# Where the second batch's filter sums run, how its second transform stage is fed, and in which steps both stand

## The chip, the cores and the metric

The kernel runs on one core of a Trainium2 chip. The metric is device time in microseconds for one execution of the whole program; the chip holds only this work. The five engines of the core are TensorE (PE, with weight loads shown as PEld), VectorE (DVE), ScalarE (ACT), GpSimd (POOL) and SyncE (SP, which here only issues DMAs).

## The reference

Two operations follow each other. The first mixes along the sequence with a filter in the frequency domain, the second is a feed-forward block with hard-swish. All is float32.

```python
# x: (8, 3008, 256); filt_r, filt_i: (1505, 256)
X = np.fft.rfft(x, axis=1)
Y = X * (filt_r + 1j * filt_i)[None, :, :]
y = np.fft.irfft(Y, n=3008, axis=1).reshape(8 * 3008, 256)
# w_in: (256, 2048), w_out: (2048, 256)
h = y @ w_in
g = h * np.clip(h + 3.0, 0.0, 6.0) / 6.0
out = g @ w_out
```

## The kernel before

**The transform** is a two-factor one, 3008 = 47 x 64. For each of the 8 batches, five kinds of unit are run:

- `a_unit(b, c)`, eight per batch: the first stage. Input pieces (47 rows in each half of the partitions) are multiplied by the table `wa`. It takes two PSUM banks. ScalarE copies the result; `z_store` writes it to the DRAM tensor `z_d`.
- `t2_load(b, c)`, six per batch: SP loads a tile of four frequency groups back from `z_d`, 512 KB.
- `b_unit(b, i)`: the second stage, with a table as the stationary operand. It fills one PSUM bank for each i, 12 in a batch.
- `f_unit(b, i)` multiplies a bank by the filter (loaded by `table_load` into `ft`), giving `s1` and `s2`. `y_unit(b, i)` adds and subtracts these into `y`.
- `bi_unit(b, i)`, for two i at a time: the first inverse stage, into two banks; ScalarE copies them to the single `t3` buffer and `g_store` writes them to `g_d` from GpSimd's queue. Later `t4_load` reads `g_d`, and `n_unit(i, dh)` does the last inverse stage and writes tokens into the ring `xn`.

All of `a_unit`, `b_unit`, `bi_unit` and `n_unit` take their banks from the one pool `psF`, which has two, under the one tag `f`; they are taken in turn.

**The feed-forward block** runs over 47 blocks of 512 tokens, each in eight steps `p` over 256 of the 2048 hidden columns. It uses a seven-product scheme in place of eight products, with sums before and after. A step is a round of the last loop of the kernel: number i = 8 x block + p. In step i TensorE runs the seven up products of step i (line 575, through `product`) and the fourteen down matmuls of step i - 1 (line 651), interleaved by hand. VectorE's queue in a step is: `hswish(k, p, 1)` of the step before (line 625), the three sums of `g_sums` (632, 633, 635), the sums `up_2b` (601) and `up_3` (606), `hswish(k, p, 0)` (625), and then what the plan has put at this step's end. At the first and last step of a block five output sums come on top. Block 0 is done by plain products (`plain_up`, `plain_down`).

**The order** is written out by hand. `at(step, fn, ...)` puts a unit into the plan of a step. Units in `EARLY` (a, b, bi and n) stand after the first three up products of the step; everything else stands at the end of the step. Within one of these lists the order is that of the calls to `at`. `places(n)` gives the steps of batch n: `a_at`, `f_at`, `y_at` and `bi_at`. From the third batch on these are offsets to the batch's first block; for the second batch (n = 1) they are a list of their own, because its transform has to run in the steps 2 to 31, while block 0 to block 3 are worked on. Batch 0 is transformed before the loop starts.

**What is special in batch 1 before.** The first stage makes two half sums (h = 0, 1). From batch 2 on `a_sums` adds and subtracts them on VectorE ahead of the store. In batch 1 the halves are stored as they are, and `t2_sums` adds and subtracts them after the load, at the steps `sums_at`, two VectorE instructions for each of six tiles. The filter products of batch 1 are placed so that both operands of the `y` sums lie on the same partitions (`near(b)`): four products of 64 x 512, and the two sums run on GpSimd (lines 461 and 462). In the later batches there are three products (446 to 448) and the two sums run on VectorE (464 and 465).

Of the kernel before, what the change touches and what calls it, by code (L numbers as in the profile page):

```python
# [12 lines left out]
AXT = mybir.ActivationFunctionType  # L13
ALU = mybir.AluOpType
PSUM = bass.MemoryType.PSUM

# [12 lines left out]
P = 128  # L31
# [27 lines left out]
def _make_tables():  # L59
    a = np.arange(NA)  # L60
    c = np.arange(NC)
    wa = np.zeros((P, HC * 2 * KH + 16))
    wai = np.zeros((P, HC, TOK))
    start = np.zeros((P, 2 * P))
    for h in range(2):
        for k in range(KH):
            th = 2 * np.pi * ((a * k) % NA) / NA

            at = k // 4 * 4 + (0, 2, 1, 3)[k % 4]
            for j in range(HC):  # L70
                tw = 2 * np.pi * (((a * NC + h * HC + j) * k) % N) / N
                wa[h * 64:h * 64 + NA, j * 2 * KH + at] = np.cos(tw)
                wa[h * 64:h * 64 + NA, j * 2 * KH + KH + at] = -np.sin(tw)
            start[h * 64:h * 64 + NA, P + 4 * k + h] = np.cos(th)
            start[h * 64:h * 64 + NA, P + 4 * k + 2 + h] = -np.sin(th)
    wb = np.zeros((P, KH, P))
    wi = np.zeros((P, 4, NC))
    wf = np.zeros((P, 2, 64))
    re, im = slice(0, NC), slice(NC, P)
    for k in range(KH):  # L80
        for q in range(64):
            f, sign = (k + NA * q, 1.0) if q < 32 else (NA * (q - 31) - k, -1.0)
            th = 2 * np.pi * ((c * f) % N) / N
            cs, sn = np.cos(th), np.sin(th)
            if f in (0, NF - 1):
                sn = np.zeros(NC)
            wb[re, k, q], wb[im, k, q] = cs, sign * sn
            wb[re, k, HALF + q], wb[im, k, HALF + q] = -sn, sign * cs

    for q in range(64):  # L90
        g, sign = (q, 1.0) if q < 32 else (31 - q, -1.0)
        co, si = (f([2 * np.pi * ((j * g) % NC) / NC for j in range(HC + 1)]) for f in (np.cos, np.sin))
        ab = np.concatenate([co, np.zeros(HC - 1) if q == 63 else si[1:HC]])
        wi[q, 3], wi[HALF + q, 3] = ab, sign * ab

        at = g % 2 * 32 + (q // 2 if q < 32 else 16 + (q - 32) // 2)
        wi[at, 0], wi[HALF + at, 0] = ab, sign * ab
        cs, sn = (np.array([f(2 * np.pi * ((j * g) % NC) / NC) for j in range(HC)]) for f in (np.cos, np.sin))
        if g % 32 == 0:
            sn = np.zeros(HC)  # L100
        for r in range(0, P, HALF):
            wf[r:r + 32, g % 2, at % 32], wf[r + 32:r + 64, g % 2, at % 32] = cs, sn
            wf[r:r + 32, g % 2, 32 + at % 32], wf[r + 32:r + 64, g % 2, 32 + at % 32] = -sign * sn, sign * cs
        wi[q, 1], wi[HALF + q, 1] = ab, -ab
        wi[q, 2], wi[HALF + q, 2] = sign * ab, sign * ab
    start[:, :P] = np.eye(P)
    for j in range(HC):
        for h in range(2):
            to = slice(h * NA, (h + 1) * NA)
            for k in range(KH):  # L110
                m = 2.0 if k else 1.0
                th = 2 * np.pi * ((a * k * NC + outer(j, h) * k) % N) / N
                cs, sn = m * np.cos(th), m * np.sin(th)
                s = -1.0 if h else 1.0
                if j:
                    wai[k, j, to], wai[32 + k, j, to] = cs, -sn
                    wai[64 + k, j, to], wai[96 + k, j, to] = -s * sn, -s * cs
                else:
                    wai[h * 64 + k, j, to], wai[h * 64 + 32 + k, j, to] = cs, -sn
    direct = np.zeros((P, TC, ND))  # L120
    n = np.array([i * NC + outer(j, h) for j in range(NJ + 1) for h in range(2) for i in range(NA)])
    for k in range(KH - TC, KH):
        for q in range(64):
            th = 2 * np.pi * (((k + NA * q if q < 32 else NA * (q - 31) - k) * n) % N) / N
            direct[q, k - KH + TC], direct[HALF + q, k - KH + TC] = 2 / N * np.cos(th), -2 / N * np.sin(th)
    f = np.float32
    return wa.astype(f), (wai / N).astype(f), wb.astype(f), wi.astype(f), wf.astype(f), start.astype(f), direct.astype(f)
# [3 lines left out]
def kernel(  # L131
# [42 lines left out]
    psO = pool("psO", 1, space=PSUM)  # L174

    wa = const.tile([P, HC * 2 * KH + 16], FP32, name="wa")
    wf = const.tile([P, 2, 64], FP32, name="wf")
    wai = const.tile([P, HC, TOK], FP32, name="wai")
    wi = const.tile([P, 4, NC], FP32, name="wi")
    xs = const.tile([P, 3, XC, D], FP32, name="xs")  # L180
# [207 lines left out]
        nc.vector.tensor_tensor(out=t[:, :, 1, :], in0=t[:, :, 0, :], in1=ps, op=ALU.subtract)  # L388
        nc.vector.tensor_tensor(out=t[:, :, 0, :], in0=t[:, :, 0, :], in1=ps, op=ALU.add)  # L389

    def t2_sums(b, c):
        t = st["t2", b, c]
        u = st["t2", b, c] = t1p.tile([P, XC // 2, 2, D], FP32, name="t1")
        nc.vector.tensor_tensor(out=u[:, :, 0, :], in0=t[:, :, 0, :], in1=t[:, :, 1, :], op=ALU.add)
        nc.vector.tensor_tensor(out=u[:, :, 1, :], in0=t[:, :, 0, :], in1=t[:, :, 1, :], op=ALU.subtract)

    def z_store(b, c, q=nc.gpsimd):
        t = st.pop(("t1", b, c))[0]
        for g in range(2):
# [3 lines left out]
                            t[p0:p0 + KH, :, :, :].rearrange("p j s d -> p (j s d)"))  # L403


    def t2_load(b, c):
        t = t2p.tile([P, TC, D], FP32, name="t2").rearrange("p (v s) d -> p v s d", v=2)
        nc.sync.dma_start(t.rearrange("p v s d -> p v (s d)"),
                          z_d[b, ts(c, TC)].rearrange("(v k) r c s d -> (k r c) v (s d)", k=2))
        st["t2", b, c] = t  # L410
# [2 lines left out]

    def b_unit(b, i):
        c, r = divmod(2 * i, TC)
        if b:
            t = st.pop(("t2", b, c))
            ps = [bank(b) for k in range(2)]
            for s_ in range(2):
# [6 lines left out]
            return  # L426
        ps = bank(b).rearrange("p (u d) -> p u d", u=2)
        for u in range(2):
            nc.tensor.matmul(ps[:, u, :], st["wb", b, c][:, r + u, :],  # L429
                             st["t2", b, c][:, r + u, :], start=True, stop=True)  # L430
        st["ps", b, i] = ps

    def f_unit(b, i):
# [5 lines left out]
        s1, s2 = (pool_.tile([P, 512], FP32, name=n).rearrange("p (u d) -> p u d", u=2) for n in (n1, n2))  # L439

        re, im = slice(0, HALF), slice(HALF, P)
        if near(b):
            for s, part, to, x_ in (s1, re, re, re), (s1, re, im, im), (s2, im, re, im), (s2, im, im, re):
                nc.vector.tensor_tensor(out=s[to], in0=ps[x_], in1=f[part], op=ALU.mult)  # L444
        else:
            nc.vector.tensor_tensor(out=s1, in0=ps, in1=f, op=ALU.mult)
            nc.vector.tensor_tensor(out=s2[re], in0=ps[re], in1=f[im], op=ALU.mult)
            nc.vector.tensor_tensor(out=s2[im], in0=ps[im], in1=f[re], op=ALU.mult)
        st["y", b, i] = s1, s2


    def near(b):
        return b == 1

    def y_unit(b, i):
        s1, s2 = st["y", b, i]
        y = yp.tile([P, 2, D], FP32, name="y") if b else rp.tile([P, 512], FP32, name="r", tag="r").rearrange(
            "p (u d) -> p u d", u=2)
        re, im = slice(0, HALF), slice(HALF, P)
        if near(b):  # L460
            nc.gpsimd.tensor_tensor(out=y[re], in0=s1[re], in1=s2[re], op=ALU.subtract)
            nc.gpsimd.tensor_tensor(out=y[im], in0=s1[im], in1=s2[im], op=ALU.add)
        else:
            nc.vector.tensor_tensor(out=y[re], in0=s1[re], in1=s1[im], op=ALU.subtract)
            nc.vector.tensor_tensor(out=y[im], in0=s2[re], in1=s2[im], op=ALU.add)
        st["y", b, i] = y


# [272 lines left out]
    with tc.manual_schedule():  # L741
# [116 lines left out]
                kinds[first[n] - 7 + d] = kind  # L858

        N_AT = {"a": ((2, 4), (2, 4), (6, 6)), "A": ((4, 5), (1, 1), (4, 5)), "B": ((2, 3), (1, 1), (2, 3))}  # L860
        N_FIRST = {0: ((3, 4),), 1: ((), (2, 2), (3, 3)), 2: ((2, 2),), 3: ((1, 1),)}
        in_block = {}
        for i in range(2, len(chunks)):
            in_block.setdefault(token(i)[0] // BLK, []).append(i)
# [18 lines left out]

        def places(n):
            if n == 1:
                f_at = [12, 13, 14, 15, 19, 20, 21, 22, 26, 27, 28, 29]
                return list(range(2, NB + 2)), f_at, [f + 1 for f in f_at], [16, 17, 23, 24, 30, 31]
            k = first[n] * NP
            a_at = [k - 7 * NP + i for i in (1, 3, 5, 7, 9, 11, 13, 15)]
            f_at, y_at, bi_at = ([k - (5 - 2 * r) * NP + i for r in range(2) for i in p]  # L890
                                 for p in ((2, 3, 6, 7, 12, 13), (4, 5, 10, 11, 14, 15), (8, 14, 16)))
            return a_at, f_at, y_at, bi_at

        sums_at = [11, 11, 17, 18, 25, 25]
        prev = None
        for n in range(1, B):
            a_at, f_at, y_at, bi_at = places(n)
# [7 lines left out]
                elif n > 1:  # L905
                    at(max(prev[c + NB - 3], s - 6), x_load, n, c)
            for c in range(NT):
                s = (sums_at[c - TB] if n == 1 else f_at[2 * (c - TB)]) + 1 if c >= TB else a_at[-1] + 1
                at(s, t2_load, n, c)
                if n == 1:  # L910
                    at(sums_at[c], t2_sums, n, c)
                s = f_at[2 * (c - FB) + 1] + 1 if c >= FB else a_at[-1 if n > 1 else 3] + 1
                at(s, table_load, n, c)
            for i in range(NU):
                if i % 2 == 0:
                    at(f_at[i], b_unit, n, i)
                    at(bi_at[i // 2], bi_unit, n, i)
                    at(bi_at[i // 2], g_store, n, i)
                at(f_at[i], f_unit, n, i)
                at(y_at[i], y_unit, n, i)  # L920
            prev = a_at


# [97 lines left out]
```

## Time and profile before

| | before |
|---|---|
| median of 7 runs | 2721.74 us (2718.7 to 2722.64) |
| time of the profiled execution | 2721.74 us |
| its span, first to last instruction | 2720.0 us, clock 0.998 |
| PE busy | 2682.2 us (99%) |
| DVE busy | 2033.5 us (75%) |
| ACT busy | 1305.7 us (48%) |
| POOL busy | 407.4 us (15%) |
| DMA | 185.83 MB, mean 68 GB/s |

The span leaves 1.74 us of the profiled execution's time outside the first and last instruction. PE's busy share says only that a matmul was in flight; whether TensorE ran at its rate is seen from the length of a step. Idle time of the other engines costs nothing unless TensorE then waits for them.

### The profile page before, as it was taken

The numbers are of one execution on the slowest core, as the hardware profiler recorded it, in microseconds if no ns is written. First come the engines' busy times: TensorE is split into PE (matmuls) and PEld (weight loads), VectorE is DVE, ScalarE is ACT, GpSimd is POOL, SyncE is SP. The second block draws the span as 40 slices with busy tenths as digits, with TensorE's granted clock in tenths as the row PEclk, the third lists the DMA queues.
The fourth block names the chain that finished last, engine by engine and source line by source line (L and its number), as shares of the span: only waits on it lengthen the run. The fifth ranks groups of instructions, "written<-read, shape, count | busy, mean of one in ns | idle before, by whom it ended". The sixth has DMA issues, their size and how long they took to land.

```text
span 2720.0 us, 49001 instructions
## 1 busy us (share of the span) xinstructions
PE 2682.2 (99%) x18894; PEld 2358.7 (87%) x18894; DVE 2033.5 (75%) x3503; ACT 1305.7 (48%) x2614; POOL 407.4 (15%) x622
## 2 busy tenths in 40 slices
PE   8899999999999999999999999999999999999998
PEld 6577788988888888988889888988888988899997
DVE  7968767787777876778767787678776778766665
ACT  3344454445544454444454445445444454445443
POOL 2432311101211011110111001211012110000000
PEclk9999999999999999999999999999999999999999
DMA  8742223211232113321133212331123321110000
GB/s 232 205 113 53 58 78 86 75 42 48 79 87 73 43 49 87 87 74 36 48 88 95 68 35 51 96 89 58 36 52 98 89 65 28 43 30 17 19 9 16
DMA packets 105062, 185.83 MB, mean 68 GB/s; under 512 B 23609, under 2 KB 63225, under 8 KB 104513
## 3 DMA queue, kind: packets, MB, share of 16 engines
q1 hardware_dynamic: 87071, 137.99, 18.3%
q0 software_dynamic: 17152, 44.22, 6.2%
q8 instruction: 150, 2.46, 0.4%
q14 instruction: 83, 0.68, 0.1%
q10 hardware_dynamic: 606, 0.49, 0.1%
HBM read 110.67 MB, written 71.93 MB: 67 GB/s over the span
## 4 chain that ended last, share of the span: by engine, by line
PE 92%; DVE 5%; DMA 1%; issue 0%; ACT 0%; SPq 0%; POOL 0%; DVEq 0%; POOLq 0%
PE po L651 42%; PE al L575 23%; PE be L575 17%; PE psn L529 4%; PE psf L476 2%; PE psf L379 2%; PE psf L422 1%; DVE g L625 1%; DVE s L444 1%; PE po L346 1%; DVE g L632 0%; PE po L429 0%; DMA out_dram<-o 0%; DVE y L271 0%; DVE y L282 0%
## 5 line engine op out<-in xcount | busy, mean ns | idle before, releaser
L651 PEld LDWEIGHTS po<-w_all,g 128*128 128x128 f32 x10304 | 1362.3, 191 | 160.9 <-issue 41.7
L651 PE MATMUL po<-w_all,g 128*128 128x128 f32 x10304 | 1406.2, 276 | 4.6 <-DVE g L625 4.5
L620 ACT ACTIVATE r<-h,half_c 128x512 f32<-128x512 f32 x736 | 531.0, 722 | 348.8 <-DVE h L601 336.7
L625 DVE SCALAR_TENSOR_TENSOR g<-r,h 128x512 f32<-128x512 f32 x736 | 513.5, 698 | 212.2 <-ACT r L620 197.5
L575 PE MATMUL al<-xt,w_all 128*128 128x256 f32 x2208 | 660.7, 381 | 4.9 <-DVE h L606 4.3
L575 PE MATMUL be<-xn,w_all 128*128 128x256 f32 x1472 | 437.8, 379 | 0.0
L601 DVE TENSOR_TENSOR h<-be,s 128x512 f32<-128x512 f32 x368 | 254.2, 691 | 225.5 <-PE be L575 213.2
L575 PEld LDWEIGHTS al<-xt,w_all 128*128 128x128 f32 x2208 | 335.2, 192 | 7.4 <-DVE h L606 5.6
L575 PEld LDWEIGHTS be<-xn,w_all 128*128 128x128 f32 x1472 | 279.7, 190 | 37.9
L615 ACT ACTIVATE h<-al 128x256 f32<-128x256 f32 x368 | 141.0, 383 | 336.6 <-PE al L575 336.6
L606 DVE TENSOR_TENSOR h<-al,s 128x256 f32<-128x256 f32 x368 | 156.1, 424 | 160.9 <-PE al L575 159.7
L633 DVE TENSOR_TENSOR g<-g 128x512 f32<-128x512 f32 x368 | 255.0, 693 | 12.6
L596 ACT ACTIVATE s<-al 128x256 f32<-128x256 f32 x368 | 141.2, 384 | 206.2 <-PE al L575 204.2
L587 ACT ACTIVATE s<-be 128x256 f32<-128x256 f32 x368 | 141.1, 383 | 176.6 <-PE be L575 176.6
L575 PE MATMUL al<-xn,w_all 128*128 128x256 f32 x736 | 219.9, 381 | 0.5 <-ACT h L615 0.5
L575 PE MATMUL be<-xt,w_all 128*128 128x256 f32 x736 | 218.9, 379 | 0.0
L635 DVE TENSOR_TENSOR g<-g 128x256 f32<-128x256 f32 x368 | 169.7, 461 | 12.5
L586 ACT ACTIVATE s<-al 128x256 f32<-128x256 f32 x368 | 141.1, 383 | 71.4 <-PE al L575 71.3
L632 DVE TENSOR_TENSOR g<-g 128x256 f32<-128x256 f32 x368 | 164.3, 446 | 12.6
L402 POOL DMA_DIRECT2D z_tmp<-t x192 | 95.2, 503 | 452.2 <-DVE t L389 441.9
L575 PEld LDWEIGHTS be<-xt,w_all 128*128 128x128 f32 x736 | 139.8, 190 | 18.9
L496 POOL DMA_DIRECT2D g_tmp<-t x84 | 52.5, 630 | 645.0 <-ACT t L479 645.0
(142 smaller groups left out, 1852.4 us busy)
## 6 DMA issues: line engine op xcount, KB each, us to landing
g_tmp<-t POOLq DMA_DIRECT2D x96, 256.0 KB, 3.7
t<-g_tmp SPq DMA_DIRECT2D x188, 120.0 KB
t<-z_tmp SPq DMA_DIRECT2D x42, 512.0 KB
z_tmp<-t POOLq DMA_DIRECT2D x192, 96.0 KB, 4.0
out_dram<-o SPq DMA_DIRECT2D x321, 47.0 KB
xs<-in_x_dram SPq DMA_DIRECT2D x112, 128.0 KB
ft<-in_filt_r_dram SPq DMA_DIRECT2D x168, 64.0 KB
ft<-in_filt_i_dram SPq DMA_DIRECT2D x168, 64.0 KB
```

The source lines that it names most:

```text
L575: nc.tensor.matmul(ps, w_in[p][:, w, :], x, start=start, stop=stop, skip_group_check=True)
L586: nc.scalar.activation(out=s[:, 0, :], in_=al, func=AXT.Copy)
L587: nc.scalar.activation(out=s5, in_=be[:, 1, :], func=AXT.Copy)
L596: nc.scalar.activation(out=s[:, 1, :], in_=al, func=AXT.Copy)
L601: nc.vector.tensor_tensor(out=st["h"][0].rearrange("p (a n) -> p a n", a=2), in0=be, in1=s, op=ALU.add)
L606: nc.vector.tensor_tensor(out=st["h"][1][:, 256:512], in0=al, in1=s5, op=ALU.add)
L620: nc.scalar.activation(out=r, in_=st["h"][i], func=AXT.Relu, bias=half_c, scale=1.0 / 6.0)
L625: nc.vector.scalar_tensor_tensor(out=st["g", k, p][:, o:o + 2, :].rearrange("p a n -> p (a n)"), in0=st["r", i], scalar=1.0, in1=st["h"][i ...
L632: v.tensor_tensor(out=g[:, G1, :], in0=g[:, G3, :], in1=g[:, G22, :], op=ALU.add)
L633: v.tensor_tensor(out=g[:, G3:G2 + 1:2, :], in0=g[:, G3:G1 + 1, :], in1=g[:, G11:G11 + 1, :].broadcast_to([P, 2, 256]), op=ALU.subtract)
L635: v.tensor_tensor(out=g[:, G4, :], in0=g[:, G12, :], in1=g[:, G2, :], op=ALU.subtract)
L651: nc.tensor.matmul(st["po", k][bank][:, part, u, :], g[:, a, ts(u, P)], w_out[p][:, w, :], start=(p == 0 and n in OPENS and u == 0), stop= ...
```

## The change

The change has four parts.

1. For batch 1 the second stage contracts over all 128 partitions. `t2_load` puts real part, column and half on the partitions and the four frequency groups along the row, and a new table in `wf`, the same for all units, does the adding and subtracting of the halves inside the matmul. `t2_sums` goes. A `b_unit` is then two 128 x 128 matmuls of 256 columns for each bank, and stands at the step of its own `f_unit`, one bank at a time.
2. In batch 1 the filter uses the three products of the later batches, and the `y` sums run on VectorE.
3. The units of batch 1 are spread anew over the steps 12 to 32. Where a step has both, `y_unit` comes ahead of `f_unit`.
4. One pair of `n_unit`s moves from step 18 to step 17, and in all later batches the last `bi_unit` of each half of the batch moves from offset 16 to 17.

```diff
-    wf = np.zeros((P, 2, 64))
+    wf = np.zeros((P, 4, 64))
...
+        for h in range(2):
+            s = -1.0 if h and g % 2 else 1.0
+            wf[h:HALF:2, 2, at], wf[HALF + h::2, 2, at] = s * cs, s * sn
+            wf[h:HALF:2, 3, at], wf[HALF + h::2, 3, at] = -s * sign * sn, s * sign * cs
...
-    def t2_sums(b, c):
-        t = st["t2", b, c]
-        u = st["t2", b, c] = t1p.tile([P, XC // 2, 2, D], FP32, name="t1")
-        nc.vector.tensor_tensor(out=u[:, :, 0, :], in0=t[:, :, 0, :], in1=t[:, :, 1, :], op=ALU.add)
-        nc.vector.tensor_tensor(out=u[:, :, 1, :], in0=t[:, :, 0, :], in1=t[:, :, 1, :], op=ALU.subtract)
...
     def t2_load(b, c):
-        t = t2p.tile([P, TC, D], FP32, name="t2").rearrange("p (v s) d -> p v s d", v=2)
+        t = t2p.tile([P, TC, D], FP32, name="t2")
+        if b == 1:
+            nc.sync.dma_start(t, z_d[b, ts(c, TC)].rearrange("k r c s d -> (r c s) k d"))
+            st["t2", b, c] = t
+            return
+        t = t.rearrange("p (v s) d -> p v s d", v=2)
...
     def b_unit(b, i):
         c, r = divmod(2 * i, TC)
-        if b:
+        if b > 1:
...
-            nc.tensor.matmul(ps[:, u, :], st["wb", b, c][:, r + u, :],
-                             st["t2", b, c][:, r + u, :], start=True, stop=True)
+            k, w = (r // 2 + 2 * u, wf[:, 2:4, :].rearrange("p a m -> p (a m)")) if b else (r + u, st["wb", b, c][:, r + u, :])
+            nc.tensor.matmul(ps[:, u, :], w, st["t2", b, c][:, k, :], start=True, stop=True)
...
     def f_unit(b, i):
-        if near(b):
-            for s, part, to, x_ in (s1, re, re, re), (s1, re, im, im), (s2, im, re, im), (s2, im, im, re):
-                nc.vector.tensor_tensor(out=s[to], in0=ps[x_], in1=f[part], op=ALU.mult)
-        else:
-            nc.vector.tensor_tensor(out=s1, in0=ps, in1=f, op=ALU.mult)
+        nc.vector.tensor_tensor(out=s1, in0=ps, in1=f, op=ALU.mult)
...
     def y_unit(b, i):
-        if near(b):
-            nc.gpsimd.tensor_tensor(out=y[re], in0=s1[re], in1=s2[re], op=ALU.subtract)
-            nc.gpsimd.tensor_tensor(out=y[im], in0=s1[im], in1=s2[im], op=ALU.add)
-        else:
-            nc.vector.tensor_tensor(out=y[re], in0=s1[re], in1=s1[im], op=ALU.subtract)
+        nc.vector.tensor_tensor(out=y[re], in0=s1[re], in1=s1[im], op=ALU.subtract)
...
-        N_FIRST = {0: ((3, 4),), 1: ((), (2, 2), (3, 3)), 2: ((2, 2),), 3: ((1, 1),)}
+        N_FIRST = {0: ((3, 4),), 1: ((), (2, 2), (3, 3)), 2: ((1, 1),), 3: ((1, 1),)}
...
             if n == 1:
-                f_at = [12, 13, 14, 15, 19, 20, 21, 22, 26, 27, 28, 29]
-                return list(range(2, NB + 2)), f_at, [f + 1 for f in f_at], [16, 17, 23, 24, 30, 31]
+                return (list(range(2, NB + 2)), [12, 13, 15, 18, 19, 20, 22, 23, 26, 27, 28, 30],
+                        [14, 15, 16, 19, 21, 22, 24, 25, 27, 29, 30, 31], [16, 21, 24, 29, 31, 32])
...
-                                 for p in ((2, 3, 6, 7, 12, 13), (4, 5, 10, 11, 14, 15), (8, 14, 16)))
+                                 for p in ((2, 3, 6, 7, 12, 13), (4, 5, 10, 11, 14, 15), (8, 14, 17)))
...
-        sums_at = [11, 11, 17, 18, 25, 25]
...
-                s = (sums_at[c - TB] if n == 1 else f_at[2 * (c - TB)]) + 1 if c >= TB else a_at[-1] + 1
+                s = f_at[2 * (c - TB) + (n == 1)] + 1 if c >= TB else a_at[-1] + 1
...
             for i in range(NU):
+                if i % 2 == 0 or n == 1:
+                    at(f_at[i], b_unit, n, i)
                 if i % 2 == 0:
-                    at(f_at[i], b_unit, n, i)
                     at(bi_at[i // 2], bi_unit, n, i)
                     at(bi_at[i // 2], g_store, n, i)
+                at(y_at[i], y_unit, n, i)
+            for i in range(NU):
                 at(f_at[i], f_unit, n, i)
-                at(y_at[i], y_unit, n, i)
```

More of the change, by code (lines that the diff above doesn't have):

```diff
@@ L176 @@
     wa = const.tile([P, HC * 2 * KH + 16], FP32, name="wa")
-    wf = const.tile([P, 2, 64], FP32, name="wf")
+    wf = const.tile([P, 4, 64], FP32, name="wf")
     wai = const.tile([P, HC, TOK], FP32, name="wai")
@@ L441, in f_unit @@
         re, im = slice(0, HALF), slice(HALF, P)
-        if near(b):
-            for s, part, to, x_ in (s1, re, re, re), (s1, re, im, im), (s2, im, re, im), (s2, im, im, re):
-                nc.vector.tensor_tensor(out=s[to], in0=ps[x_], in1=f[part], op=ALU.mult)
-        else:
-            nc.vector.tensor_tensor(out=s1, in0=ps, in1=f, op=ALU.mult)
-            nc.vector.tensor_tensor(out=s2[re], in0=ps[re], in1=f[im], op=ALU.mult)
-            nc.vector.tensor_tensor(out=s2[im], in0=ps[im], in1=f[re], op=ALU.mult)
+        nc.vector.tensor_tensor(out=s1, in0=ps, in1=f, op=ALU.mult)
+        nc.vector.tensor_tensor(out=s2[re], in0=ps[re], in1=f[im], op=ALU.mult)
+        nc.vector.tensor_tensor(out=s2[im], in0=ps[im], in1=f[re], op=ALU.mult)
         st["y", b, i] = s1, s2
-    def near(b):
-        return b == 1
     def y_unit(b, i):
@@ L459, in y_unit @@
         re, im = slice(0, HALF), slice(HALF, P)
-        if near(b):
-            nc.gpsimd.tensor_tensor(out=y[re], in0=s1[re], in1=s2[re], op=ALU.subtract)
-            nc.gpsimd.tensor_tensor(out=y[im], in0=s1[im], in1=s2[im], op=ALU.add)
-        else:
-            nc.vector.tensor_tensor(out=y[re], in0=s1[re], in1=s1[im], op=ALU.subtract)
-            nc.vector.tensor_tensor(out=y[im], in0=s2[re], in1=s2[im], op=ALU.add)
+        nc.vector.tensor_tensor(out=y[re], in0=s1[re], in1=s1[im], op=ALU.subtract)
+        nc.vector.tensor_tensor(out=y[im], in0=s2[re], in1=s2[im], op=ALU.add)
         st["y", b, i] = y
@@ L907 @@
             for c in range(NT):
-                s = (sums_at[c - TB] if n == 1 else f_at[2 * (c - TB)]) + 1 if c >= TB else a_at[-1] + 1
+                s = f_at[2 * (c - TB) + (n == 1)] + 1 if c >= TB else a_at[-1] + 1
                 at(s, t2_load, n, c)
-                if n == 1:
-                    at(sums_at[c], t2_sums, n, c)
                 s = f_at[2 * (c - FB) + 1] + 1 if c >= FB else a_at[-1 if n > 1 else 3] + 1
```

## The prediction, made before the result was known

> **What bounds the kernel now.** I read four views: the page's busy times and chain, the windows of single steps, the timeline of two steps, and the rows of single tiles.
>
> ```profile
> PE 2682.2 (99%) x18894; PEld 2358.7 (87%) x18894; DVE 2033.5 (75%) x3503; ACT 1305.7 (48%) x2614; POOL 407.4 (15%) x622
> PE 92%; DVE 5%; DMA 1%; issue 0%; ACT 0%; SPq 0%; POOL 0%; DVEq 0%; POOLq 0%
> ```
>
> TensorE bounds the whole; 5% of the chain lies on VectorE. To find where, I cut the timeline at the first `al<-xn` matmul of each step (step = 8 x block + p) and asked for windows from cut to cut (columns: length, then busy PE, PEld, DVE, ACT, POOL).
>
> ```profile
> 242.49:250.49 8.00, 7.03 (x44) 5.77 (x43) 7.35 (x11) 2.97 (x7) 2.87 (x2) 1.00 0.31 96
> 250.49:259.15 8.66, 8.63 (x60) 6.09 (x59) 7.99 (x12) 2.98 (x7) 2.86 (x2) 1.00 0.23 62
> 259.15:267.81 8.66, 7.03 (x44) 5.77 (x43) 7.99 (x12) 2.98 (x7) 2.87 (x2) 1.00 0.00 0
> 267.81:276.21 8.40, 8.40 (x52) 6.09 (x51) 6.47 (x11) 4.17 (x9) 3.78 (x4) 1.00 0.48 127
> 453.37:459.52 6.15, 6.15 (x44) 5.79 (x43) 4.83 (x9) 3.46 (x8) 1.97 (x4) 1.00 0.27 67
> 465.67:473.03 7.36, 7.36 (x60) 5.88 (x59) 4.92 (x9) 2.97 (x7) 0.00 (x0) 1.00 0.63 147
> 672.83:680.20 7.37, 7.37 (x53) 5.92 (x51) 4.94 (x9) 4.52 (x10) 1.23 (x2) 1.00 0.26 65
> ```
>
> The last three are undisturbed: a plain step takes 6.15 us; a `b_unit` of two banks, a `bi_unit` or an `a_unit` adds 1.22 each (7.37); an `n_unit` adds 1.11 (two make a step of 8.38). The first four are steps 20 to 23 of the second batch. Steps 20 and 22 hold no transform matmul and take 8.00 and 8.66 instead of 6.15, with VectorE almost always busy. Over steps 11 to 32 (168.60 to 346.46, 177.86 us) the undisturbed lengths sum to 22 x 6.15 + 6 n_units x 1.11 + 6 bi x 1.22 + 6 b x 1.22 = 156.6. The rest, **21.2 us, is stall**: 0.67, 1.71, 2.15, 2.42, 1.04 in steps 12 to 16; 1.85, 1.29, 2.51, 1.03 in 20 to 23; 1.79, 1.27, 2.51, 1.02 in 27 to 30. That is what this change can win. Batches from the third on show no stall.
>
> ```profile
> 243.67 1.27 POOL L461 TENSOR_TENSOR y<-s,s 64x512 f32<-64x512 f32 x1 [10.35 <-DVE s L444]
> 244.27 1.21 DVE L625 SCALAR_TENSOR_TENSOR g<-r,h 128x512 f32<-128x512 f32 x1
> 245.01 1.60 POOL L462 TENSOR_TENSOR y<-s,s 64x512 f32<-64x512 f32 x1
> 245.52 1.37 DVE L632 TENSOR_TENSOR g<-g 128x256 f32<-128x256 f32 x1
> ...
> 249.06 0.70 PE L575 MATMUL al<-xt,w_all 128*128 128x256 f32 x2 [0.68 <-DVE h L606]
> ```
>
> While GpSimd sums `y`, L625 takes 1.21 instead of 0.69 and L632 1.37 instead of 0.42: 0.52 + 0.95 = 1.47 us per filter unit. The end of the delayed row is L606, and TensorE waits for it.
>
> **The change, part by part.** *VectorE's sums.* Removed: 12 `t2_sums` instructions (0.68 undisturbed) and one of four filter products per unit (12 x 0.69). Added: two `y` sums per unit, 24 x 0.69.
>
> ```profile
> L446 DVE TENSOR_TENSOR s<-psf,ft x72: 682/684/692, 472.0 to 2330.7; 128x512 f32<-128x512 f32 x72
> L464 DVE TENSOR_TENSOR y<-s x72: 686/687/689, 485.6 to 2344.0; 64x512 f32<-64x512 f32 x72
> ```
>
> So 60 extra instructions before and 60 after: VectorE's own work is unchanged, and only two things matter, the contention and the spread. Contention: 12 x 1.47 = 17.6 us of VectorE time goes. The Trainium skill, "SBUF — State Buffer", section "SBUF: two separate sides", says that a VectorE instruction with two SBUF inputs and a GpSimd one exclude each other for the whole instruction. By that rule each unit could block VectorE for 1.28 + 1.55 us (L461, L462), 33.9 us in all; I take the measured 17.6, and the stall caps the gain at 21.2 anyway. The rule also speaks against the new `y` sums: they read SBUF twice, and what stays on GpSimd can block them. That is the weight sums of L293 (until 190.2 us, while steps 12 and 13 run; L625 there takes 0.94) and `t_sums` (four of 0.73, in steps 17 and 25). I add 0.65 us to VectorE's load in steps 12 and 13; in 25 the step lasts 8.38 us and hides it.
>
> Spread: units stand at f = 12, 13, 15, 18, 19, 20, 22, 23, 26, 27, 28, 30 with three instructions, y at 14, 15, 16, 19, 21, 22, 24, 25, 27, 29, 30, 31 with two. Steps 15, 19, 22, 27 and 30 carry five (y ahead of f in the queue); no other more than three. From the timeline of step 19 I measure what a step allows. With S the start of the next step, L625 runs at S-1.68, the extras begin at S-1.08 and take 0.715 each. Then follow L625, L632, L633, L635, L601, L606, which end at S+2.2 to 2.4 + 0.715n. TensorE asks for L606 at S+4.72+X, X being the transform work at that step's head. Check on before: n = 4 and 1.47 of contention give 2.2 + 2.86 + 1.47 = 6.5 against 4.72: stall 1.8; measured 1.85, 1.71, 1.79. After, n = 3 ends at 4.3 to 4.6: no stall even with X = 0. In steps 12 and 13 it ends at 5.0 to 5.2, under 5.58. n = 5 ends at 5.8 to 6.0. After 15 and 30 a bi_unit follows (limit 5.94 or later): nothing. After 19, 22 and 27 a b_unit follows (5.58): 0.3 each, **0.9**, and VectorE stays 0.7 late for one step.
>
> *bi_units behind a filter unit.* A bi_unit takes both `psf` banks; its second half waits until the filter unit before it has read its bank. Steps 23 and 30 before show this: filter done at S+2.41, step 1.03 long. After: steps 16 and 31 follow a five-step, whose filter ends at S+2.50: 1.1 each. Steps 21, 24 and 29 follow a three-step that is 0.7 late, filter done at S+1.78 instead of the S+1.40 at which the bank is wanted: 0.4 each. Together **3.4**. The `y` it needs comes earlier: S+0.35.
>
> *TensorE's second stage.* Before: eight 64x32 matmuls in eight tiles at once, 1.22 per pair of units, switching included. After: four 128x128 matmuls of 256 columns. L575's two records of that shape stand 0.43 us apart from the next pair, so 1.72 per pair, and the weight load (0.19) hides behind the matmul as there. 6 x 0.50 = **3.0 us more**. The skill's "TensorEngine Tiling (Array Packing)", "Theoretical Speedup" and "Key Properties", gives eight such tiles up to eight times the rate, but a drain at each change of mode. By packing alone (0.86) the change would cost 6 x 0.86 = 5.2; the row has the drain in it (1.22), so I use the row.
>
> *Loads.* The z load has pieces of 1 KB, not 2 KB. The trace's packets take 46 and 84 ns at the median: 512 KB over 16 engines is 1.5 instead of 1.3 us. The chain of waits has the first such load from 171.59 to 175.58; its reader stands at about 178.3 (step 12), so 2.7 us cover it. If cover is gone, each us late is one us of TensorE idle, once. `wf` grows by 64 KB: under 0.5 us in the start-up, beside other loads: nothing. SP's later loads (steps 14, 19, 21) are used five to eight steps later, also the filter tables moved with them; the g stores that GpSimd issues have no `y` sums ahead of them any more, and the one `t3` buffer sees consecutive bi_units at 31, 32 as before at 30, 31. The n_units from step 18 to 17: their rows were loaded from 173.7, used after 218; same length. The rows that the last bi_units store (steps 32, 81 and so on) are loaded again at 36, 83 and so on; a g store lands in 3.7 us, and the load starts after it. Nothing for all of these; each would cost its own delay once if the next use came within a step.
>
> *The later batches.* The last bi_unit of each half moves from 16 to 17. In the queue of the changed program this puts it, in five batches, into the same step as the next batch's first `a_unit`, just ahead of it. Both take both banks.
>
> ```profile
> 674.22 0.21 PEld L476 LDWEIGHTS psf<-y,wi 64*64 64x64 f32 x8 [0.33 <-issue]
> ...
> 675.37 1.08 ACT L479 ACTIVATE t<-psf 128x512 f32<-128x512 f32 x2 [0.66 <-PE psf L476]
> ```
> ```profile
> 94.60 1.81 PE L379 MATMUL psf<-xs,wa 47*64 47x256 f32 x16
> ...
> 95.32 0.63 PEld L379 LDWEIGHTS psf<-xs,wa 47*64 47x64 f32 x14 [0.53 <-ACT xn L535]
> ```
>
> The step of the first fence starts at 672.83, so ScalarE has freed the second bank at S+3.63. The second fence shows an a_unit caught behind a bank: it went on when the bank was read and needed 1.02 us from there. So the collision ends at S+4.7, against S+3.63 for the two units one after the other: 1.05 each, **5.2 us**. At one more place two n_units precede the bi_unit: the second bank is read 0.7 later than wanted, **0.7**. The other places change nothing (a plain step takes it up).
>
> **Sum:** -21.2 + 0.9 + 3.4 + 3.0 + 5.2 + 0.7 = -8.0 us. The profiled execution took 2721.74 (span 2720.0 and 1.74 around it), which is also the median of the seven: 2721.7 - 8.0 = **2713.7 us**. A difference of 0.2%, 5.4 us, is about what a measurement here can tell from none.
>
> **The rivals.** (A) *The collision costs little* (ScalarE frees the banks while TensorE does something else): gain 13 to 14, 2708. Against it: TensorE's queue is in order, and the second fence. (B) *VectorE still bounds the five-steps*, say 1.8 each as the four-steps did, with the delay passed on: 5 x 1.8 instead of 0.9 puts the time at about 2722. For it: five instructions are more than four; against it: the 1.47 of contention is more than one instruction. (C) *The collisions are the change's price*, slower: if the late a_unit also holds its bank for `a_sums` into the next step and each of five places costs p, the sum turns at p = 2.6 us and is 5.4 slower at p = 3.7: then 2727 or more. For it: that step also carries the block-end sums on VectorE (6.05 busy of 7.37). Against it: TensorE's delay gives VectorE as much time.
>
> **How the numbers follow.** Forecast 0.64 (own range 2710 to 2718), A 0.13, B 0.13, C 0.10. Ends for the unknowns: collisions 0.6 to 1.8 each (3 to 9), waits of bi_units 1 to 6, first load 0 to 2. So 2707.5 to 2720.5 holds eight in ten. Faster by over 0.2% (under 2716.3): 0.67; within 0.2%: 0.22; slower: 0.11.
>
> **What would show it.** Steps 12, 13, 14 at 7.0, 7.0, 6.15; steps 20, 23, 28 at about 7.0 to 7.3; 16 and 31 at about 8.5; no L625 above 0.95. The five steps with bi and a at 9.6. I am wrong if steps 15 to 31 keep lengths above 8 without a bi_unit, or if the step at 81 is near 8.6 or above 11.

## The result, and the profile after

The changed kernel takes **2714.25 us** (median of 13 runs, 2712.27 to 2717.53), the kernel before 2721.02 us (33 runs, 2718.7 to 2727.32). The ratio is 0.9974, with a 95% interval from 0.9967 to 0.9981: 6.8 us faster by the medians. The forecast was 2713.7 us, faster by 8.0 us.

The page of the kernel after, its busy times and the chain of work that ended last by engine:

```profile
PE 2679.4 (99%) x18846; PEld 2368.2 (87%) x18846; DVE 2023.5 (75%) x3503; ACT 1306.2 (48%) x2614; POOL 372.1 (14%) x598
PE 96%; DVE 3%; DMA 1%; ACT 0%; issue 0%; POOL 0%; SPq 0%; POOLq 0%; DVEq 0%
```

VectorE's share of the chain falls from 5% to 3%; its busy time falls by 10.0 us although it runs as many instructions as before (3503). So the instructions got shorter on average.

The windows of single steps of the kernel after, cut at the same instruction as before: steps 20 to 23, then the plain step 48, then steps 80 and 81 (columns: window, length, busy PE, PEld, DVE, ACT, POOL, clock, DMA share, GB/s).

```profile
234.53:242.01 7.48, 7.28 (x48) 6.55 (x47) 6.80 (x12) 2.98 (x7) 0.00 (x0) 1.00 0.24 67
242.01:249.70 7.69, 7.69 (x52) 6.09 (x51) 6.52 (x12) 4.06 (x9) 1.25 (x2) 1.00 0.80 227
249.70:256.71 7.01, 7.01 (x48) 6.55 (x47) 5.32 (x10) 2.97 (x7) 0.00 (x0) 1.00 0.27 89
256.71:264.20 7.49, 7.28 (x49) 6.55 (x47) 6.81 (x12) 2.98 (x7) 0.00 (x0) 1.00 0.00 0
439.67:445.81 6.14, 6.14 (x44) 5.78 (x43) 4.69 (x9) 3.45 (x8) 1.97 (x4) 1.00 0.32 81
659.17:665.32 6.15, 6.15 (x45) 5.79 (x44) 4.94 (x9) 3.46 (x8) 0.00 (x0) 1.00 0.00 0
665.32:674.94 9.62, 8.94 (x68) 6.60 (x67) 6.12 (x14) 4.66 (x10) 1.92 (x3) 1.00 0.24 60
```

Three things are to be seen. First, steps 20 to 23 take 7.48, 7.69, 7.01 and 7.49 us where they took 8.00, 8.66, 8.66 and 8.40. Second, step 22 has the new `b_unit` and no wait: 7.01 is 6.15 + 0.86, so two full matmuls cost what was reckoned. Third, step 81, which now holds a `bi_unit` and an `a_unit`, takes 9.62: with step 80 that is 15.77 instead of 14.74.

The timeline of VectorE in a step with five extra instructions (step 19, extras from 233.57 to 237.10). The numbers of these lines are five lower than before: L620 is the old L625, L627 the old L632, L601 the old L606.

```profile
233.57 0.69 DVE L459 TENSOR_TENSOR y<-s 64x512 f32<-64x512 f32 x1
...
236.41 0.69 DVE L451 TENSOR_TENSOR s<-psf,ft 64x512 f32<-64x512 f32 x1
237.14 0.69 DVE L620 SCALAR_TENSOR_TENSOR g<-r,h 128x512 f32<-128x512 f32 x1
237.87 0.42 DVE L627 TENSOR_TENSOR g<-g 128x256 f32<-128x256 f32 x1
...
240.12 0.41 DVE L601 TENSOR_TENSOR h<-al,s 128x256 f32<-128x256 f32 x1
```

L620 is back at 0.69 (it was 1.21) and L627 at 0.42 (it was 1.37). L601 ends at 240.53, 6.00 us after the next step began at 234.53; TensorE wanted it at 5.58, by the prediction's own reckoning (4.72 and the 0.86 of a `b_unit`).

To compare kernels I use sums of step lengths in the profiled executions, in two stretches, because the time up to step 8 differs from execution to execution (last section). Steps 8 to 10 take 25.0 us in all nine kernels. The stretch 11 to 32 holds the second batch's second stage, the stretch from 33 to 374 the later batches.

| kernel | steps 11 to 32 | steps 33 to 374 |
|---|---|---|
| before | 177.86 us | 2352.15 us |
| after | 164.75 us | 2358.08 us |
| E1 before, shift to 17 alone | 177.88 us | 2358.09 us |
| E2 after, shift undone | 164.70 us | 2352.39 us |
| E3 after, sums on GpSimd | 170.84 us | 2358.05 us |
| E4 after, old places | 170.75 us | 2357.91 us |
| E5 before, new second stage alone | 175.61 us | 2351.84 us |
| E6 after, shift undone, step 30 turned | 163.58 us | 2352.05 us |
| E7 before, shift in first halves alone | 177.85 us | 2352.80 us |

So the change wins 13.1 us in the second batch and gives 5.9 us back in the later ones.

### The profile page after: what moved, and what is told of

It reads as the page before. It is cut to its first block, busy times and chain, and to the rows that moved or that the text cites. A ratio compares the mean times of both kernels' runs of the same rounds, so it can differ in the third digit from the quotient of the medians.

```text
span 2712.5 us, 48871 instructions
## 1 busy us (share of the span) xinstructions
PE 2679.4 (99%) x18846; PEld 2368.2 (87%) x18846; DVE 2023.5 (75%) x3503; ACT 1306.2 (48%) x2614; POOL 372.1 (14%) x598
## 4 chain that ended last, share of the span: by engine, by line
PE 96%; DVE 3%; DMA 1%; ACT 0%; issue 0%; POOL 0%; SPq 0%; POOLq 0%; DVEq 0%
PE po L646 43%; PE al L570 24%; PE be L570 17%; PE psn L524 4%; PE psf L471 2%; PE psf L385 2%; PE psf L428 1%; PE po L352 1%; PE po L437 0%; PE psf L437 0%; DVE g L620 0%; DVE y L288 0%; DVE y L277 0%; DVE y L290 0%; DVE w_all L293 0%; PE al L779 0%
## 5 line engine op out<-in xcount | busy, mean ns | idle before, releaser
L620 DVE SCALAR_TENSOR_TENSOR g<-r,h 128x512 f32<-128x512 f32 x736 | 507.3, 689 | 208.8 <-ACT r L615 194.3
L601 DVE TENSOR_TENSOR h<-al,s 128x256 f32<-128x256 f32 x368 | 156.2, 424 | 166.6 <-PE al L570 165.5
L628 DVE TENSOR_TENSOR g<-g 128x512 f32<-128x512 f32 x368 | 255.9, 695 | 12.6
L630 DVE TENSOR_TENSOR g<-g 128x256 f32<-128x256 f32 x368 | 170.6, 464 | 12.5
L627 DVE TENSOR_TENSOR g<-g 128x256 f32<-128x256 f32 x368 | 156.7, 426 | 12.6
```

Source lines behind the costliest of these rows:

```text
L601: nc.vector.tensor_tensor(out=st["h"][1][:, 256:512], in0=al, in1=s5, op=ALU.add)
L620: nc.vector.scalar_tensor_tensor(out=st["g", k, p][:, o:o + 2, :].rearrange("p a n -> p (a n)"), in0=st["r", i], scalar=1.0, in1=st["h"][i ...
L627: v.tensor_tensor(out=g[:, G1, :], in0=g[:, G3, :], in1=g[:, G22, :], op=ALU.add)
L628: v.tensor_tensor(out=g[:, G3:G2 + 1:2, :], in0=g[:, G3:G1 + 1, :], in1=g[:, G11:G11 + 1, :].broadcast_to([P, 2, 256]), op=ALU.subtract)
L630: v.tensor_tensor(out=g[:, G4, :], in0=g[:, G12, :], in1=g[:, G2, :], op=ALU.subtract)
```

## The experiments

**E1: the shift alone, on the kernel before.**

```diff
-                                 for p in ((2, 3, 6, 7, 12, 13), (4, 5, 10, 11, 14, 15), (8, 14, 16)))
+                                 for p in ((2, 3, 6, 7, 12, 13), (4, 5, 10, 11, 14, 15), (8, 14, 17)))
```

> The kernel before with only the last bi_unit of each half-batch moved from offset 16 to 17. Collision theory: in five steps (81, 129, 177, 225, 273) the bi_unit stands just ahead of an a_unit that wants the same two banks; each of these steps takes 9.6 us and the pair of steps 1.0 us more than before, step 257 another 0.7. So 5.9 us slower than before, about 2727. Rival A (the banks come free in time): within 1 us of before.

Measured: 2725.81 us (11 runs) against 2720.71, ratio 1.0020 (1.0011 to 1.0029). The later batches take 5.94 us more, the second batch the same. The windows of steps 80 and 81 of E1:

```profile
670.55:676.70 6.15, 6.15 (x45) 5.79 (x43) 4.94 (x9) 3.47 (x8) 0.00 (x0) 1.00 0.00 0
676.70:686.32 9.62, 8.94 (x68) 6.60 (x67) 6.04 (x14) 4.67 (x10) 1.93 (x3) 1.00 0.24 62
```

The steps are those of the changed kernel to the hundredth. All five places (81, 129, 177, 225, 273) have 9.62, and step 257 goes from 8.38 to 10.28, 0.68 more than the 1.22 of the `bi_unit` that it took over. The timeline of step 81 in the kernel after shows the cause:

```profile
666.71 1.09 PE L471 MATMUL psf<-y,wi 64*64 64x512 f32 x8
667.83 1.09 ACT L474 ACTIVATE t<-psf 128x512 f32<-128x512 f32 x2 [0.63 <-PE psf L471]
668.48 0.19 PEld L385 LDWEIGHTS psf<-xs,wa 47*64 47x64 f32 x2 [1.57 <-ACT t L474]
668.48 1.57 PE L385 MATMUL psf<-xs,wa 47*64 47x256 f32 x16 [0.68 <-ACT t L474]
668.97 0.63 PEld L385 LDWEIGHTS psf<-xs,wa 47*64 47x64 f32 x14 [0.30 <-ACT t L474]
```

The brackets give the idle time before the instruction and what ended it. The first matmuls of the `a_unit` wait for ScalarE's first copy of the `bi_unit`, the rest for its second, which frees the second bank at 668.92. Rival A, that the collision costs little, falls.

**E2: the changed kernel without the shift.**

```diff
-                                 for p in ((2, 3, 6, 7, 12, 13), (4, 5, 10, 11, 14, 15), (8, 14, 17)))
+                                 for p in ((2, 3, 6, 7, 12, 13), (4, 5, 10, 11, 14, 15), (8, 14, 16)))
```

> The changed kernel with the shift to offset 17 undone and all else kept. Collision theory: 5.9 us faster than the changed kernel, about 2708.3, with steps 80 and 81 back at 7.37 each and the second batch's steps as in the changed kernel. If the shift helped the second batch in some way that I did not see, less than that.

Measured: 2706.60 us (5 runs), ratio to before 0.9949 (0.9936 to 0.9961). The stretch of the later batches is 5.69 us shorter than in the changed kernel, and the second batch's is the same (164.70 against 164.75). So the shift costs nearly what was reckoned (5.9) and brings the second batch nothing.

**E7: the shift in the first half of each batch alone**, on the kernel before, where no `a_unit` stands in the same step.

```diff
             f_at, y_at, bi_at = ([k - (5 - 2 * r) * NP + i for r in range(2) for i in p]
                                  for p in ((2, 3, 6, 7, 12, 13), (4, 5, 10, 11, 14, 15), (8, 14, 16)))
+            bi_at[2] += 1
```

> The kernel before with the shift from 16 to 17 in the first half of each batch only, where no a_unit stands in the same step. Collision theory: steps 64 and 65 exchange their lengths (6.15 and 7.37), step 257 takes 0.7 more; 0.7 us slower in sum, not to be told from before by time. If the shift costs by itself (a later g store, the block's end on VectorE), some 5 us.

Measured: 2720.15 us (10 runs) against 2720.25, ratio 0.9997 (0.9988 to 1.0007). The later batches take 0.65 us more, all of it in step 257. Steps 64 and 65 exchange their lengths. The move as such is free; it costs where another unit in the same step takes the same two banks (an `a_unit` in E1, two `n_unit`s in step 257).

**E3: the y sums back on GpSimd, everything else as changed.**

```diff
     def f_unit(b, i):
-        nc.vector.tensor_tensor(out=s1, in0=ps, in1=f, op=ALU.mult)
...
+        if b == 1:
+            for s, part, to, x_ in (s1, re, re, re), (s1, re, im, im), (s2, im, re, im), (s2, im, im, re):
+                nc.vector.tensor_tensor(out=s[to], in0=ps[x_], in1=f[part], op=ALU.mult)
...
     def y_unit(b, i):
+        if b == 1:
+            nc.gpsimd.tensor_tensor(out=y[re], in0=s1[re], in1=s2[re], op=ALU.subtract)
+            nc.gpsimd.tensor_tensor(out=y[im], in0=s1[im], in1=s2[im], op=ALU.add)
```

> The changed kernel with the second batch's y sums back on GpSimd (and so four filter products a unit), at the changed places. Contention theory: each filter step costs VectorE 4 products and 1.5 us of blocked L625 and L632 (L620 and L627 by this kernel's own lines), as before; steps behind one filter step wait 1 us, those behind two in a row 1.6, a plain one 2. Over the second batch some 9 to 13 us more than the changed kernel: 2723 to 2727. Rival (the new places did it, the engine does not matter): within 3 us of the changed kernel.

Measured: 2718.35 us (11 runs), ratio to before 0.9990 (0.9981 to 0.9999); the second batch takes 6.1 us more than in the changed kernel. That is more than the rival allows, and well below the 9 to 13 that I expected. The contention is there again, as the timeline of step 19 shows:

```profile
229.56 1.26 POOL L464 TENSOR_TENSOR y<-s,s 64x512 f32<-64x512 f32 x1 [9.31 <-DVE s L451]
230.16 1.20 DVE L628 SCALAR_TENSOR_TENSOR g<-r,h 128x512 f32<-128x512 f32 x1
230.89 1.60 POOL L465 TENSOR_TENSOR y<-s,s 64x512 f32<-64x512 f32 x1
231.40 1.37 DVE L635 TENSOR_TENSOR g<-g 128x256 f32<-128x256 f32 x1
```

Where I was wrong is in when the sums come. GpSimd's own timeline over steps 19 to 22:

```profile
230.89 1.60 POOL L465 TENSOR_TENSOR y<-s,s 64x512 f32<-64x512 f32 x1
248.05 1.26 POOL L499 DMA_DIRECT2D g_tmp<-t  x2 [15.56 <-ACT t L482]
249.37 1.27 POOL L464 TENSOR_TENSOR y<-s,s 64x512 f32<-64x512 f32 x1
```

The next unit's products were done at 238.8, but its sums start at 249.37: in GpSimd's queue they stand behind the `g_store` of step 21, which waits for ScalarE. So step 20 has no contention and takes 7.19 us, not the 8.66 of two filter steps in a row with it. I had priced every filter step alike and left out the queue that the sums stand in. E3 also gives VectorE 12 instructions fewer than the changed kernel (four products a unit instead of three products and two sums), so its 6.1 us are what the contention costs less what those 12 would have cost.

**E4: the old places, with the sums on VectorE.**

```diff
             if n == 1:
-                return (list(range(2, NB + 2)), [12, 13, 15, 18, 19, 20, 22, 23, 26, 27, 28, 30],
-                        [14, 15, 16, 19, 21, 22, 24, 25, 27, 29, 30, 31], [16, 21, 24, 29, 31, 32])
+                f_at = [12, 13, 14, 15, 19, 20, 21, 22, 26, 27, 28, 29]
+                return list(range(2, NB + 2)), f_at, [f + 1 for f in f_at], [16, 17, 23, 24, 30, 31]
...
-        N_FIRST = {0: ((3, 4),), 1: ((), (2, 2), (3, 3)), 2: ((1, 1),), 3: ((1, 1),)}
+        N_FIRST = {0: ((3, 4),), 1: ((), (2, 2), (3, 3)), 2: ((2, 2),), 3: ((1, 1),)}
```

> The changed kernel with the second batch's units at their old steps (filter at 12 to 15, 19 to 22, 26 to 29, y one step later, bi at 16, 17, 23, 24, 30, 31; the n_units back at 18). Then three steps in a row carry five VectorE instructions. Spread theory: the second of them waits 0.5, the third 1.1, the bi_unit behind them 2.0 for its bank: 3.6 a group where the changed kernel has 1.7. So 4 to 8 us slower than the changed kernel, about 2720. Rival (only the contention mattered): within 2 us of it.

Measured: 2720.16 us (11 runs), ratio to before 0.9997 (0.9989 to 1.0006); the second batch takes 6.0 us more than in the changed kernel. The windows of steps 14, 15 and 16 of E4, behind one, two and three steps in a row with five extras:

```profile
187.65:195.14 7.49, 7.27 (x48) 6.54 (x47) 6.78 (x12) 2.98 (x7) 0.00 (x0) 1.00 0.29 74
195.14:203.28 8.14, 7.55 (x49) 6.54 (x47) 7.41 (x13) 2.99 (x7) 0.00 (x0) 1.00 0.19 63
203.28:212.51 9.23, 8.42 (x52) 6.09 (x51) 7.68 (x13) 4.67 (x10) 1.30 (x2) 1.00 0.39 98
```

Against 7.01, 7.01 and 7.37 these wait 0.48, 1.13 and 1.86; expected were 0.5, 1.1 and 2.0. Each of the three waits; one five-step costs 0.48, and in a row the delay adds up, in step 16 on the `bi_unit`'s bank. Step 17 then takes 8.06, 0.69 over a step with one `bi_unit`.

**E5: the new second stage alone**, sums on GpSimd and all at the old places. Against the kernel before:

```diff
-        if b:
+        if b > 1:
...
-                if n == 1:
-                    at(sums_at[c], t2_sums, n, c)
```

with the new table, the load by halves and one `b_unit` a step, as in the change.

> The kernel before with only the new second stage: loads with real part, column and half on the partitions, one 128x128 table, no t2_sums; y sums on GpSimd with four products, all at the old places, the late bi_units at offset 16. Theory: 12 VectorE sums fewer, but TensorE works 3.0 us more, and most filter steps keep their length, since it is set by VectorE and the contention (8.66). Only step 12 and the head of each group gain: 1 to 3 us faster than before, about 2719.5. Rival (the removed t2_sums are the gain): 7 to 9 us faster.

Measured: 2717.48 us (11 runs), ratio to before 0.9990 (0.9981 to 0.9999); the second batch is 2.25 us shorter. The windows of steps 20 to 23 of E5 are the old ones:

```profile
243.07:251.06 7.99, 7.31 (x48) 6.66 (x47) 7.34 (x11) 2.98 (x7) 2.85 (x2) 1.00 0.10 31
251.06:259.72 8.66, 7.90 (x49) 6.54 (x47) 7.99 (x12) 2.98 (x7) 2.86 (x2) 1.00 0.46 123
259.72:268.38 8.66, 7.89 (x49) 6.54 (x48) 7.99 (x12) 2.98 (x7) 2.86 (x2) 1.00 0.00 0
268.38:276.78 8.40, 8.40 (x52) 6.09 (x51) 6.47 (x11) 4.16 (x9) 3.78 (x4) 1.00 0.46 125
```

TensorE does more in the two steps that held no transform before (20 and 22: 7.31 and 7.89 busy instead of 7.03), and their length does not move: VectorE, as busy as before (7.34 and 7.99), sets it. Only steps 12, 13, 19 and 26 are shorter, by 1.03, 0.53, 0.35 and 0.35. The rival, that the removed `t2_sums` are the gain, falls.

**E6: E2, with the filter products ahead of the y sums in step 30.**

```diff
-                at(y_at[i], y_unit, n, i)
+                if (n, i) != (1, 10):
+                    at(y_at[i], y_unit, n, i)
             for i in range(NU):
                 at(f_at[i], f_unit, n, i)
+            if n == 1:
+                at(y_at[10], y_unit, n, 10)
```

> The changed kernel with the shift to offset 17 undone and, in step 30 alone, the filter products ahead of the y sums. Theory: the bank that the bi_unit of step 31 waits for is read 1.4 us earlier, step 31 takes 7.4 instead of 8.6. So 1.1 us faster than the same kernel without it and 7 us faster than the changed one: about 2707.2. Rival (step 31 waits for VectorE's L601-like sums and not for the bank): no difference to the kernel without it.

Measured: 2706.88 us (5 runs), ratio to before 0.9944 (0.9931 to 0.9956); from E2 (0.9949) the time cannot tell it, the trace can. Step 31 of the kernel after, then of E6:

```profile
317.98 2.30 PE L471 MATMUL psf<-y,wi 64*64 64x512 f32 x8
...
319.20 0.19 PEld L471 LDWEIGHTS psf<-y,wi 64*64 64x64 f32 x4 [1.03 <-DVE s L451]
```
```profile
319.73 1.09 PE L471 MATMUL psf<-y,wi 64*64 64x512 f32 x8
```

The second half of the `bi_unit` no longer waits 1.03 us for the last filter product, and the step goes from 8.57 in E2 to 7.43. E6 is the shortest of all kernels by its steps. It and E2 beat both the kernel before and the changed one.

## Why the prediction was right

The forecast was that the stall of VectorE in the second batch goes and that collisions in the later batches give part of it back. Both happened, at the places named. Point by point:

- **What bounds the second batch.** 21.2 us of stall was the upper limit. Of it 4.3 were to stay, and TensorE's second stage was to add 3.0 of work. In the kernel after, the undisturbed lengths of steps 11 to 32 sum to 159.6 (156.6 and the 3.0), and the steps take 164.75, so 5.1 of stall stayed.
- **Sums and spread.** Both were needed. With neither, E5 takes 175.61 us; the places alone (E3) give 170.84, the engine alone (E4) 170.75, both 164.75: 4.8 and 4.9 alone, 10.9 together. The new second stage gives 2.25 more. Behind a step with three extras there is no stall when no `bi_unit` follows: 13, 14, 19 and 27 take 7.01, 6.19, 7.01 and 7.01.
- **Contention.** Reckoned at 12 x 1.47 = 17.6 us of VectorE time. These are the two rows hit, over the window from 176 to 333 us, before and then after (busy us, mean ns):

```profile
L625 DVE SCALAR_TENSOR_TENSOR g<-r,h 128x512 f32<-128x512 f32 x39 | 34.0, 872 | 7.3 <-ACT r L620 6.9
L632 DVE TENSOR_TENSOR g<-g 128x256 f32<-128x256 f32 x19 | 15.9, 839 | 0.7
```
```profile
L620 DVE SCALAR_TENSOR_TENSOR g<-r,h 128x512 f32<-128x512 f32 x42 | 29.6, 704 | 6.6 <-ACT r L615 5.3
L627 DVE TENSOR_TENSOR g<-g 128x256 f32<-128x256 f32 x21 | 9.2, 438 | 0.7
```

  Before they are 39 x 0.182 + 19 x 0.414 = 15.0 us over the undisturbed 690 and 425, after 0.9. So 14 us went rather than 17.6: not every unit cost the full 1.47. The forecast of the time did not suffer, because it was made with the stalls and not with this. Of the signs named, "no L625 above 0.95" was just missed: one L620, in step 12, takes 0.99, beside the weight sums that GpSimd makes there, and the step has no stall.
- **Five-steps.** Reckoned at 0.3 each, measured at 0.47 (steps 20, 23 and 28: 7.48, 7.48, 7.49 against 7.01). The term that was too small is the row from the extras to L601: L601 ends 6.00 us after the step's start, the upper end of my 5.8 to 6.0, and TensorE takes up its work another 0.05 later. Rival B had 1.8 each and falls; E4 shows that it is the third in a row that comes to something like it (1.86 in step 16, where the wait is for the `bi_unit`'s bank). The signs named 7.0 to 7.3 for these steps; 7.48 lies above.
- **bi_units behind a filter unit.** Reckoned at 1.1 twice and 0.4 three times; measured 1.2 (8.58 twice, against 7.37) and 0.32 (7.69). E6 took away the one in step 31 and with it the wait.
- **Steps 17 and 25.** They take 8.55 and 8.49, 0.17 and 0.11 over the 8.38 of a step with two `n_unit`s. The prediction named the cause and put it at nothing: GpSimd's `t_sums` (L563) run there, and the step's 8.38 us were to hide them. In step 17 of the kernel after:

```profile
213.32 0.69 DVE L460 TENSOR_TENSOR y<-s 64x512 f32<-64x512 f32 x1
215.25 0.73 POOL L563 TENSOR_TENSOR xt<-xn 128x256 f32<-128x256 f32 x1 [5.94 <-ACT xn L530]
215.30 1.22 DVE L628 TENSOR_TENSOR g<-g 128x512 f32<-128x512 f32 x1
216.55 0.88 DVE L630 TENSOR_TENSOR g<-g 128x256 f32<-128x256 f32 x1
218.15 0.97 PEld L646 LDWEIGHTS po<-w_all,g 128*128 128x128 f32 x8 [0.26 <-DVE o L701]
```

  With two `y` sums ahead of them, L628 and L630 meet the `t_sums` and take 1.22 and 0.88 instead of 0.69 and 0.43; TensorE then waits 0.26 for the output sum L701 behind them. In E3, which has no `y` sums in VectorE's queue, the same two rows of step 17 take 0.69 and 0.42 and both steps 8.38. The sign "lengths above 8 without a bi_unit" was drawn too wide: these two steps would have 8.38 with no stall at all.
- **TensorE's second stage.** Four full matmuls a pair at 0.43 each: a `b_unit` adds 0.86 and two of them 1.72, as the 7.01 of each such step shows. Reckoning by tiles without the drain would have made it 5.2 instead of 3.0.
- **Loads.** Step 12 takes 7.01, its undisturbed length, so the load with 1 KB pieces was in time.
- **Collisions.** Reckoned at 1.05 five times and 0.7 once, 5.9 in sum. Measured 1.03 and 0.68, in the kernel after and in E1; the stretch grows by 5.93 and 5.94. Rival C needed 2.6 or more at each place and falls.

From step 8 to the end the profiled executions differ by 6.65 us. The forecast of 8.0 misses it by 1.3: 0.8 in the second batch's remaining stall, and 0.5 in the last step and output (21.34 us before, 21.88 after), which the prediction left alone. That stretch takes 21.9 us in the four kernels that sum the second batch's `y` on VectorE (after, E2, E4, E6) and 21.3 to 21.4 in the other five; no run tells why. The medians differ by 6.8 and so miss it by 1.2. The time up to step 8, which the forecast took as fixed, moves by up to 5.8 us between single executions, so how near the medians come is in part luck; the steps are the better test.

## What to carry to other kernels

Where one engine bounds, cut the trace at a repeating instruction, take the undisturbed length of each kind of step from a stretch without waits, and sum: the difference is all that a change there can win. When work is spread, count what each step's queue gets and how late its last instruction may be, since a step absorbs up to a limit and steps in a row pass the rest on. And look at every unit that a change moves for what it now stands next to in the same buffers: here a move by one step took back 5.9 of 13.1 us.

## What was not expected of the hardware

- GpSimd's share of the contention depends on when its instructions come, which its queue decides. In E3, sums that were ready at 238.8 ran at 249.4, and the wait they cause fell in other steps than planned.
- The time from the first instruction to step 8 is not steady. In the nine profiled executions it lies between 140.22 us (E4) and 146.04 us (E5), and these two share all of the program up to there; from step 8 on the steps of two kernels with the same plan agree to 0.01 us nearly everywhere. So a difference of a few us between single executions tells nothing here, and the steps do. The granted clock is part of what varies: between 50 and 100 us it was 0.93 in E5 and E6, which have the two longest starts, and 1.00 in E4 and in the kernel before. It is not all: the kernel before has the clock of E4 in its start, and needs 143.57 us. The rest was not tested.
